# The sign bit of converted weights from a two-slope ACT function, and weight rounding at the head of a unit, in pooled attention with two MLPs

## The chip, the cores and the metric

The kernel runs on one core of one Trainium2 chip. The metric is the device time of one execution in microseconds. The core has five engines that run their own instructions in order: TensorE (PE, with the weight loads shown as PEld), VectorE (DVE), ScalarE (ACT), GpSimd (POOL) and SyncE (SP), which here only issues DMAs. They wait for each other through semaphores.

## What is computed

Attention over queries that are pooled in pairs, then an MLP with a squared ReLU, then a gated MLP without an activation:

```
q_pool = mean of two neighbouring queries            # (2, 8, 576, 64)
attn   = softmax(q_pool @ k.T / sqrt(64)) @ v        # k, v: (2, 8, 1152, 64)
x      = attn as (1152, 512)
g      = s * relu(x @ w_in)**2 + b                   # w_in: (512, 2048)
x2     = g @ w_out                                   # (2048, 512)
out    = ((x2 @ w_a) * (x2 @ w_b)) @ w_out2          # w_a, w_b: (512, 1536); w_out2: (1536, 512)
```

The weights of both MLPs arrive as float64. The result is float32.

## The kernel before

All products run on TensorE in a float32 form that rounds its operands, so each operand is split into a rounded part `h` and the rest `l`, and a product takes three matmuls: h·h, h·l, l·h (`mm3`, L542).

Attention comes first, for eight pairs of heads. Its instructions on all engines are put in order by hand: the list `SCHED` names the steps of one pair, with primes for those that run one or more pairs late, and `CV` in it is one step of weight conversion. Ten such steps lie in the last pairs and behind them.

The first MLP has 16 units of weights (columns of `w_in` or rows of `w_out`, 1024 values per partition each), the second has 12 (m = 0 to 11, a 512x128 block of `w_a` and one of `w_b`). Units are numbered through, so the second MLP begins with unit 16. A unit of the second MLP is two groups of matmuls: w = 0 makes x2·w_a, which ACT copies out as `at`; w = 1 makes x2·w_b, which VectorE multiplies by `at` into `ab`. A group is 12 blocks of three matmuls of 384 columns. The last stage multiplies `ab`, split again, by all of `w_out2`.

Each unit of weights is converted from float64 by six steps of a generator (`conv_all`, L155). The four of `conv_bits` (L136 to L146) build float32 bits in `f`: (1) ACT scales the high word, read as a float32, by 2^-112 (L139); (2) VectorE shifts it left by three (L141), which loses the sign; (3) VectorE ORs in the three top bits of the low word (L143); (4) VectorE ORs in the sign of the high word (L145). The two of `conv_split` round on GpSimd: `wh` (L150) and the rest `wl` (L152). Step five also issues the DMA of a later unit's raw weights (`unit_load`, L125), from SP's queue, into one of two `raw` buffers, which is free when the last reader of its old contents has finished.

`w_out2` is converted by a generator of its own, `w2_conv` (L711), in 12 blocks kf with 512 values per partition, through one buffer `w2raw` and one buffer `f2`. Its first load, `w2_load(0)`, is issued when the generator is first advanced.

What sets the order in the second MLP (loop at the end of the function): for each m, behind the matmuls and evacuations of w = 0, six steps of `conv` (rounding of unit m+17, then the bits of unit m+18), and behind those of w = 1 six steps of `w2_steps` (bits and rounding of block m). `unit_next` at the head of m takes the rounded weights that were made during the unit before. The rounded weights have two buffers, so `wh` of a unit can be written when TensorE has finished the unit two before. The memory of the first MLP is given back at `m1.close()` (L695), and the pool `m2`, which holds `w2raw`, `f2`, `ab` and the rounded `w_out2`, is laid over it.

Of the kernel before, what the change touches and what calls it, by code (L numbers as in the profile page):

```python
# [8 lines left out]
F32 = mybir.dt.float32  # L9
# [3 lines left out]
AF = mybir.ActivationFunctionType  # L13
ALU = mybir.AluOpType
# [27 lines left out]
def kernel(  # L42
# [14 lines left out]
    nc = tc.nc  # L57
# [52 lines left out]
    for up, c, u in order1:  # L110
        if up:
            w = w_in[:, c * 512 + u * 256:c * 512 + (u + 1) * 256]
        else:
            w = w_out[c * 512:(c + 1) * 512, u * 256:(u + 1) * 256]
# [21 lines left out]
    def conv_bits(f, raw):  # L136
        words = raw.bitcast(I32).rearrange("p (n t) -> p n t", t=2)
        lo, hi = words[:, :, 0], words[:, :, 1]
        nc.scalar.activation(out=f.bitcast(F32), in_=hi.bitcast(F32), func=AF.Copy, scale=2.0 ** -112)  # L139
        yield  # L140
        nc.vector.tensor_scalar(out=f, in0=f, scalar1=3, scalar2=None, op0=ALU.logical_shift_left)  # L141
        yield
        nc.vector.scalar_tensor_tensor(out=f, in0=lo, scalar=29, in1=f, op0=ALU.logical_shift_right, op1=ALU.bitwise_or)  # L143
        yield
        nc.vector.scalar_tensor_tensor(out=f, in0=hi, scalar=-(1 << 31), in1=f, op0=ALU.bitwise_and, op1=ALU.bitwise_or)  # L145
        yield  # L146

    def conv_split(f, h, l):
        f = f.bitcast(F32)
        nc.gpsimd.tensor_scalar(out=h, in0=f, scalar1=1.0, scalar2=0.0, op0=ALU.mult, op1=ALU.add)  # L150
        yield
        nc.gpsimd.tensor_tensor(out=l, in0=f, in1=h.bitcast(F32), op=ALU.subtract)  # L152
        yield

    def conv_all():  # L155
        for i in range(len(units)):
            f = cv_ps[i % len(cv_ps)].tile([128, 1024], I32, tag="f", name="f")
            yield from conv_bits(f, raw_t.pop(i))
            unit_load()
            p = sp_ps[i % 2]  # L160
            h, l = (p.tile([128, 1024], F32R, tag=f"w{x}", name=f"w{x}") for x in "hl")
            sp_t.append((h, l))
            yield from conv_split(f, h, l)

    conv = conv_all()

    def conv_step(n=1, steps=conv):
        for _ in range(n):
            next(steps, None)

    def unit_next():
        return sp_t.pop(0)
# [369 lines left out]
    def mm3(parts, w, x, first, last):  # L542

        (wh, wl), (xh, xl) = w, x
        for z, (a, c) in enumerate([(wh, xh), (wh, xl), (wl, xh)]):
            o = 0
            for ps in parts:
                n = ps.shape[-1]
                nc.tensor.matmul(ps, a, c[:, o:o + n], start=(first and z == 0), stop=(last and z == 2))  # L549
                o += n  # L550

    with tc.manual_schedule():
# [35 lines left out]
        def ps_tile():  # L588
            p = ps_pools[n_ps[0] % 2]
            n_ps[0] += 1  # L590
            return [p.tile([128, 512], F32, tag=f"ps{i}", name=f"ps{i}")[:, 0:NT // 3] for i in range(3)]
# [111 lines left out]
        def w2_at(x, kf):  # L703
            return w2[x][:, kf]

        def w2_load(kf):
            raw = m2_p.tile([128, DM], I64, tag="w2raw", name="w2raw")
            nc.sync.dma_start(out=raw, in_=w_out2[kf * 128:(kf + 1) * 128, :])
            return raw

        def w2_conv():  # L711
            raw = w2_load(0)
            for kf in range(KF2):
                f = m2_p.tile([128, DM], I32, tag="f2", name="f2")
                yield from conv_bits(f, raw)
                if kf + 1 < KF2:
                    raw = w2_load(kf + 1)
                yield from conv_split(f, w2_at(0, kf), w2_at(1, kf))

        w2_steps = w2_conv()  # L720
        ab = m2_p.tile([128, KF2, NT], F32, tag="ab", name="ab")
        tiles = [(b, j) for b in range(B) for j in range(4)] + [None]
        orow = [out[b * SP:b * SP + 512].rearrange("(p j) d -> p j d", j=4) for b in range(B)]
# [4 lines left out]
        def ab_split(i):  # L728
            if i >= len(chunks):
                return  # L730
            t, z = chunks[i]
            kc = slice(4 * z, 4 * z + 4)
            a = abt[i] = sp_ps[i // 2 % 2].tile([128, 2, 4, 128], F32R, tag=f"w{'hl'[i % 2]}", name="abt")
            if t is not None:
                b, j = t
                split(a[:, 0], a[:, 1], ab[:, kc, b * SP + cols(j):b * SP + cols(j) + 128], nc.scalar, nc.vector)
            else:
                for b in range(B):
                    c = slice(b * NX, (b + 1) * NX)
                    split(a[:, 0, :, c], a[:, 1, :, c], ab[:, kc, b * SP + 256:b * SP + 256 + NX], nc.scalar, nc.vector)  # L740

        for m in range(KF2):
            wh, wl = (x.rearrange("p (w k f) -> p w k f", w=2, k=4) for x in unit_next())
            if m == KF2 - 1:
                ab_split(0)
                ab_split(1)
            at = a_p.tile([128, NT], F32, tag="at", name="at")
            for w in range(2):
                ps = ps_tile()
                for kk in range(KD):  # L750
                    mm3(ps, (wh[:, w, kk], wl[:, w, kk]), (x2h[:, kk], x2l[:, kk]), kk == 0, kk == KD - 1)
                for i in range(3):
                    c = slice(i * NT // 3, (i + 1) * NT // 3)
                    if w == 0:
                        nc.scalar.copy(out=at[:, c], in_=ps[i])  # L755
                    else:
                        nc.vector.tensor_tensor(out=ab[:, m, c], in0=ps[i], in1=at[:, c], op=ALU.mult)
                conv_step(6, w2_steps if w else conv)
        conv_step(1, w2_steps)

        for i, (t, z) in enumerate(chunks):
# [49 lines left out]
```

## Time and profile before

| | |
|---|---|
| median of 3 runs | 716.09 us (715.78 to 716.54) |
| profiled execution: time / span | 716.33 us / 714.5 us |
| PE busy | 694.3 us, 97%, 4302 matmuls |
| DVE busy | 489.1 us, 68%, 911 instructions |
| ACT busy | 366.7 us, 51%, 859 |
| POOL busy | 385.8 us, 54%, 388 |
| share of the chain that ended last | PE 83%, DVE 9%, ACT 3%, POOL 2% |

Times inside the execution are counted from the start of the span. Busy time of TensorE is not its peak: matmuls are pipelined, and their durations overlap, so the distance between starts says how fast it goes. The granted clock is given as a share of full speed, 1.00 being 2.4 GHz and 0.50 1.2 GHz. Attention ends at about 271 us, the first MLP at about 475, the second MLP's units at 630 and TensorE's last matmul at 704.8 us.

### The profile page before, as it was taken

Reading aid. Unit: us, or ns where it says so; the run is one execution under the profiler, and the core shown is the slowest. Engines: PE = TensorE matmul, PEld = TensorE weight load, DVE = VectorE, ACT = ScalarE, POOL = GpSimd, SP = SyncE. Lnnn points to the kernel's source line nnn. Section 1 sums busy time; section 2 is a strip of 40 time slices with the busy share of each in tenths; the row PEclk is TensorE's granted clock in tenths of the full one; section 3 lists DMA queues with packets and bytes.
Section 4 is the critical chain, followed back from the end, with each engine's and each line's share of the span. In section 5 each row is a group of like instructions: output and inputs, shape, how many; then the busy total and the mean of one; then the engine's idle time right before and its main releaser. Section 6 shows DMA issues by size and latency. Waiting matters only on the chain.

```text
span 714.5 us, 11549 instructions
## 1 busy us (share of the span) xinstructions
PE 694.3 (97%) x4302; PEld 665.3 (93%) x4302; DVE 489.1 (68%) x911; ACT 366.7 (51%) x859; POOL 385.8 (54%) x388
## 2 busy tenths in 40 slices
PE   7999999999999989999999999999899999999994
PEld 6899999999999989999999999999899999988883
DVE  5999999999999995786386577675555546342220
ACT  5998999999999983454333224122113131222220
POOL 4879798888879764785545454231544352410000
PEclk9999999999999999999999999999999999999998
DMA  6122120312121004231313131223252430100000
GB/s 224 35 67 67 36 77 25 100 32 69 34 67 35 1 8 149 81 118 65 113 60 119 60 118 59 93 85 118 89 175 90 148 119 30 60 16 30 29 30 29
DMA packets 32443, 52.90 MB, mean 74 GB/s; under 512 B 1924, under 2 KB 15492, under 8 KB 32388
## 3 DMA queue, kind: packets, MB, share of 16 engines
q1 hardware_dynamic: 32258, 52.04, 22.2%
q8 instruction: 34, 0.56, 0.3%
q14 instruction: 21, 0.17, 0.1%
q10 hardware_dynamic: 130, 0.13, 0.1%
HBM read 49.81 MB, written 2.36 MB: 73 GB/s over the span
## 4 chain that ended last, share of the span: by engine, by line
PE 83%; DVE 9%; ACT 3%; POOL 2%; issue 2%; DMA 1%; ACTq 0%; POOLq 0%
PE ps L549 47%; PE ps L769 9%; PE pv L434 8%; PE t L400 7%; PE s L325 6%; PE s L332 3%; DVE p3l L418 2%; DVE sm L351 2%; PE t L270 1%; ACT p3h L412 1%; PE t L290 1%; DVE sm L348 1%; DVE xs L453 1%; DMA w2raw<-in_moe_w_out_dram 1%; ACT x L275 1%
## 5 line engine op out<-in xcount | busy, mean ns | idle before, releaser
L400 PE MATMUL t<-ident,e 128*128 128x128 f32 x648 | 98.5, 275 | 3.3 <-DVE p2l L418 1.5
L383 POOL TENSOR_SCALAR e<-e,sm 128x1152 f32<-128x1152 f32 x72 | 88.5, 1231 | 11.5 <-DVE sm L378 6.7
L400 PEld LDWEIGHTS t<-ident,e 128*128 128x128 f32 x648 | 75.2, 140 | 13.6 <-DVE p3l L418 2.1
L653 POOL TENSOR_SCALAR r<-r,sb_s,sb_b 128x384 f32<-128x384 f32 (+1 forms) x46 | 44.5, 979 | 54.7 <-DVE r L650 54.7
L141 DVE TENSOR_SCALAR f<-f 128x1024 int32<-128x1024 int32 (+1 forms) x40 | 30.5, 763 | 60.0 <-ACT f L139 59.9
L152 POOL TENSOR_TENSOR wl<-f,wh 128x1024 fp32r<-128x1024 f32 x28 | 69.8, 2492 | 2.2
L348 DVE TENSOR_REDUCE sm<-s 128x1 f32<-128x768 f32 x72 | 68.3, 948 | 2.0 <-PE s L325 2.0
L418 DVE TENSOR_TENSOR p3l<-t,p3h 128x512 fp32r<-128x512 f32 (+1 forms) x120 | 64.3, 554 | 7.0 <-ACT p3h L412 4.6
L549 PE MATMUL ps<-x2h,wl 128*128 128x384 f32 x288 | 66.3, 338 | 2.0 <-POOL wl L152 2.0
L769 PE MATMUL ps<-w2h,abt 128*128 128x512 f32 x216 | 67.4, 393 | 0.0
L549 PE MATMUL ps<-x2h,wh 128*128 128x384 f32 x288 | 66.2, 338 | 0.4 <-POOL wh L150 0.4
L367 ACT ACTIVATE e<-s,sm 128x768 f32<-128x768 f32 x72 | 66.5, 923 | 0.0
L549 PE MATMUL ps<-x2l,wh 128*128 128x384 f32 x288 | 66.0, 337 | 0.0
L755 ACT COPY at<-ps 128x384 f32<-128x384 f32 x36 | 14.9, 487 | 97.2 <-PE ps L549 97.2
L150 POOL TENSOR_SCALAR w2h<-f 128x512 fp32r<-128x512 f32 x12 | 8.2, 683 | 94.7 <-DVE f L145 94.7
L412 ACT CAST p3h<-t 128x512 fp32r<-128x512 f32 (+1 forms) x120 | 56.2, 485 | 6.0 <-PE t L400 3.7
L150 POOL TENSOR_SCALAR wh<-f 128x1024 fp32r<-128x1024 f32 x28 | 32.8, 1171 | 45.4 <-PE ps L549 39.8
L549 PEld LDWEIGHTS ps<-x2h,wl 128*128 128x128 f32 x288 | 51.7, 190 | 2.3 <-POOL wl L152 2.3
L549 PEld LDWEIGHTS ps<-x2h,wh 128*128 128x128 f32 x288 | 51.9, 190 | 0.7 <-POOL wh L150 0.7
L98 DVE TENSOR_TENSOR abt<-ab,abt 128x512 fp32r<-128x512 f32 (+1 forms) x30 | 19.9, 699 | 46.9 <-ACT abt L93 46.9
L549 PEld LDWEIGHTS ps<-x2l,wh 128*128 128x128 f32 x288 | 51.8, 189 | 0.0
L647 ACT ACTIVATE r<-ps 128x384 f32<-128x384 f32 (+1 forms) x46 | 20.2, 505 | 60.0 <-PE ps L549 60.0
(106 smaller groups left out, 1906.0 us busy)
## 6 DMA issues: line engine op xcount, KB each, us to landing
raw<-in_moe_w_in_dram SPq DMA_DIRECT2D x8, 1024.0 KB, 5.5
raw<-in_moe_w_out_dram SPq DMA_DIRECT2D x8, 1024.0 KB, 5.0
raw<-in_moe_w_a_dram SPq DMA_DIRECT2D x12, 512.0 KB, 3.6
raw<-in_moe_w_b_dram SPq DMA_DIRECT2D x12, 512.0 KB, 4.7
w2raw<-in_moe_w_out_dram SPq DMA_DIRECT2D x12, 512.0 KB, 3.3
vn<-in_v_dram SPq DMA_DIRECT2D x8, 576.0 KB, 3.9
kn<-in_k_dram SPq DMA_DIRECT2D x7, 576.0 KB, 3.9
qn<-in_q_dram SPq DMA_DIRECT2D x7, 512.0 KB, 3.7
```

The costliest lines, as they stand in the source:

```text
L152: nc.gpsimd.tensor_tensor(out=l, in0=f, in1=h.bitcast(F32), op=ALU.subtract)
L325: nc.tensor.matmul(ps[:, c, 0:384], w, x[:, c * 384:(c + 1) * 384], start=(z == 0), stop=(z == len(pr) - 1))
L348: nc.vector.reduce_max(small(g)[:, 0:1], SPS[g, 0][:, :, 0:384], axis=AX.XY)
L367: nc.scalar.activation(out=e_tile(g)[:, 0:768].rearrange("p (a c) -> p a c", a=2), in_=SPS.pop((g, 0))[:, :, 0:384], func=AF.Exp, bias=m[: ...
L383: nc.gpsimd.tensor_scalar(out=e, in0=e, scalar1=m[:, 6:7], scalar2=1.0, op0=ALU.mult, op1=ALU.mult)
L400: nc.tensor.transpose(ps[:, i * 128:(i + 1) * 128], E[g][:, (c0 + i) * 128:(c0 + i + 1) * 128], ident)
L412: nc.scalar.copy(out=p_dst(g)[0][:, c0:c0 + n], in_=p_src(g, z))
L418: nc.vector.tensor_tensor(out=l, in0=p_src(g, z), in1=h.bitcast(F32), op=ALU.subtract)
L434: nc.tensor.matmul(ps[:, 0:N], V[n, hd][:, c].rearrange("p a d -> p (a d)"), p, start=(t == 0), stop=(t == 2 * NC - 1))
L549: nc.tensor.matmul(ps, a, c[:, o:o + n], start=(first and z == 0), stop=(last and z == 2))
L653: nc.gpsimd.tensor_scalar(out=r2, in0=r2, scalar1=sb_s, scalar2=sb_b, op0=ALU.mult, op1=ALU.add)
L769: nc.tensor.matmul(ps, a[:, x, kk], w2_at(c, kf), start=(kf == 0 and y == 0), stop=(kf == KF2 - 1 and y == 2))
```

## The change

The first conversion step uses ACT's function Prelu, whose slope for negative inputs is alpha times that for positive ones. With alpha = 2^32 a negative value's exponent is 32 higher, which is bit 28 of the word, and the shift left by three brings this bit to the sign's place. The fourth step, the OR of the sign on VectorE, is gone; its `yield` stays, so that the count of steps is as before.

In the second MLP, two conversion steps (the rounding of the next unit's weights, with the DMA of a later unit's raw weights) stand at the head of a unit and no longer behind its first group, where four steps are left. The load of the first block of `w_out2` is issued when the generator is made, ahead of the loop and of `ab`'s allocation.

```diff
     def conv_bits(f, raw):
         words = raw.bitcast(I32).rearrange("p (n t) -> p n t", t=2)
         lo, hi = words[:, :, 0], words[:, :, 1]
-        nc.scalar.activation(out=f.bitcast(F32), in_=hi.bitcast(F32), func=AF.Copy, scale=2.0 ** -112)
+
+        nc.scalar.activation(out=f.bitcast(F32), in_=hi.bitcast(F32), func=AF.Prelu, scale=2.0 ** -112, alpha=2.0 ** 32)
         yield
         nc.vector.tensor_scalar(out=f, in0=f, scalar1=3, scalar2=None, op0=ALU.logical_shift_left)
         yield
         nc.vector.scalar_tensor_tensor(out=f, in0=lo, scalar=29, in1=f, op0=ALU.logical_shift_right, op1=ALU.bitwise_or)
         yield
-        nc.vector.scalar_tensor_tensor(out=f, in0=hi, scalar=-(1 << 31), in1=f, op0=ALU.bitwise_and, op1=ALU.bitwise_or)
         yield
...
-        def w2_conv():
-            raw = w2_load(0)
+        def w2_conv(raw):
             for kf in range(KF2):
...
-        w2_steps = w2_conv()
+        w2_steps = w2_conv(w2_load(0))
         ab = m2_p.tile([128, KF2, NT], F32, tag="ab", name="ab")
...
         for m in range(KF2):
             wh, wl = (x.rearrange("p (w k f) -> p w k f", w=2, k=4) for x in unit_next())
+            conv_step(2)
             if m == KF2 - 1:
...
-                conv_step(6, w2_steps if w else conv)
+                conv_step(*((6, w2_steps) if w else (4,)))
         conv_step(1, w2_steps)
```

## Rows read from the trace of the kernel before

**Rows 1.** Table by stretches: length, busy PE, PEld, DVE, ACT, POOL; clock; DMA, GB/s.

```profile
179.46:211.83 32.37, 32.26 (x241) 30.97 (x241) 30.76 (x74) 29.82 (x80) 27.38 (x34) 1.00 0.18 56
211.83:244.47 32.64, 32.42 (x241) 30.98 (x241) 31.55 (x75) 30.96 (x81) 27.66 (x34) 1.00 0.06 20
244.47:271.07 26.60, 24.79 (x180) 23.09 (x179) 24.95 (x56) 21.22 (x54) 19.01 (x22) 1.00 0.12 41
...
287.01:475.00 187.99, 187.93 (x1079) 186.66 (x1078) 130.76 (x179) 66.75 (x126) 97.16 (x75) 1.00 0.25 85
...
500.13:509.85 9.72, 7.34 (x32) 6.70 (x32) 5.96 (x8) 0.68 (x1) 7.64 (x6) 0.82 0.49 163
509.85:630.08 120.23, 120.23 (x695) 120.23 (x695) 56.49 (x81) 27.47 (x50) 47.18 (x35) 1.00 0.28 93
```

**Rows 2.** Chain that ended last, in order of time: start, length, what.

```profile
264.30 1.68 DVE f L145
...
280.68 1.65 DVE f L145
...
488.38 5.67 DMA w2raw<-in_moe_w_out_dram
494.13 0.67 ACT f L139
...
501.26 3.21 POOL wl L152
```

**Rows 3.** Timeline, TensorE at the stall: start, duration, idle time before it in brackets.

```profile
500.13 0.69 PE L549 MATMUL ps<-x2h,wl 128*128 128x384 f32 x3
501.23 0.80 PE L549 MATMUL ps<-x2h,wh 128*128 128x384 f32 x3 [0.41 <-POOL wh L150]
...
504.51 1.03 PE L549 MATMUL ps<-x2h,wl 128*128 128x384 f32 x3 [1.96 <-POOL wl L152]
...
509.85 0.68 PE L549 MATMUL ps<-x2h,wh 128*128 128x384 f32 x3
```

**Rows 4.** Table by stretches, two microseconds behind the gap.

```profile
506.00:508.00 2.00, 2.00 (x8) 2.00 (x7) 0.19 (x1) 0.00 (x0) 1.64 (x2) 0.50 0.68 202
```

**Rows 5.** Timeline, SP's queue of DMA issues.

```profile
487.36 0.37 SPq L132 DMA_DIRECT2D raw<-in_moe_w_a_dram  x1
...
488.38 8.73 SPq L708 DMA_DIRECT2D w2raw<-in_moe_w_out_dram  x2
```

**Rows 6.** Timeline, VectorE from the first MLP's end through unit 16.

```profile
476.92 3.38 DVE L98 TENSOR_TENSOR x2l<-xacc,x2h 128x384 fp32r<-128x384 f32 x3
...
486.06 1.23 DVE L145 SCALAR_TENSOR_TENSOR f<-raw,f 128x1024 int32<-128x1024 int32 x1
488.02 1.49 DVE L757 TENSOR_TENSOR ab<-ps,at 128x384 f32<-128x384 f32 x3 [0.73 <-PE ps L549]
```

**Rows 7.** Timeline, GpSimd in an undisturbed unit of the second MLP.

```profile
520.86 0.62 POOL L150 TENSOR_SCALAR w2h<-f 128x512 fp32r<-128x512 f32 x1 [9.11 <-DVE f L145]
...
523.97 2.42 POOL L152 TENSOR_TENSOR wl<-f,wh 128x1024 fp32r<-128x1024 f32 x1
```

**Rows 8.** Timeline, TensorE beside the two L145 of the chain.

```profile
266.19 0.31 PE L434 MATMUL pv<-p3l,v 128*128 128x320 f32 x1
266.73 0.63 PE L400 MATMUL t<-ident,e 128*128 128x128 f32 x4 [0.23 <-DVE p2l L418]
...
283.10 0.42 PE L549 MATMUL ps<-xa_h,wl 128*128 128x288 f32 x2
283.73 0.53 PE L549 MATMUL ps<-xa_h,wh 128*128 128x288 f32 x2 [0.20 <-DVE r L650]
```

**Rows 9.** Groups by line: busy time, mean ns of one, idle time before and its releaser.

```profile
L145 DVE SCALAR_TENSOR_TENSOR f<-raw,f 128x1024 int32<-128x1024 int32 x28 | 36.7, 1310 | 0.9
...
L139 ACT ACTIVATE f<-raw 128x1024 f32<-128x1024 f32 x28 | 32.3, 1154 | 2.4 <-POOL wl L152 2.4
...
L93 ACT ACT_TABLE_LOAD x1 | 1.3, 1283 | 0.7 <-PEq L795 0.7
```

## The prediction

> **What bounds the kernel now.** I read the table by stretches first, because the mean busy share says nothing about which stage a change touches. From the first MLP on TensorE is the bound: in 287 to 475 us it is busy for 187.93 of 187.99 us at a granted clock of 1.00, and in 510 to 630 us for all 120.23 us [rows 1]. In there a cheaper VectorE step is worth nothing by itself: VectorE is idle for half of the later stretch. One stretch stands out, 500.13 to 509.85 us: TensorE 7.34 of 9.72 us, clock 0.82 [rows 1].
>
> Second, the chain of waits, to see what holds TensorE there. It runs from the first DMA of `w2raw` (issued 488.38, landed 494.05) over the ACT conversion at 494.13 and VectorE and GpSimd to `wl` at 501.26, ready at about 504.5 [rows 2]. Third, TensorE's own order of time. A block of three matmuls, one 128x384 tile by three parts, comes every 0.52 us; from the block at 500.13 to the one at 509.85 there are ten steps, which should take 5.20 us and take 9.72 [rows 3]. So 4.52 us are lost at this one place. Of that, 9.72 - 7.34 = 2.38 us is idle time, and the other 2.14 us is the clock: after the gap ahead of 504.51 it is granted at 0.50, the 1.2 GHz level, in 506 to 508 us [rows 3, 4].
>
> Earlier the chain also runs over the operation that is removed, L145: at 264.30 for 1.68 us, at the end of the attention, and at 280.68 for 1.65 us, in the first unit of the first MLP [rows 2]. These two places and the stall at 500 us are where the change can act. What TensorE does elsewhere is its own work.
>
> **The stall at 500 us, part by part.** The change moves `w2_load(0)` to ahead of all steps of the second MLP. Before, SP's queue holds the raw load of a later unit first. That load waits for its buffer, whose last reader is L145 of unit 18 (486.06 + 1.23 = 487.29), goes at 487.36, and `w2_load(0)` follows at 488.38 [rows 5, 6]. After, nothing of this loop is ahead of it in SP's queue. It must still wait for memory of the first MLP that `w2raw` is laid over; the last user of that memory which I see is `x2l<-xacc` on VectorE, ending at 476.92 + 3.38 = 480.30 [rows 6]. So the issue moves from 488.38 to 480.30 at the latest, and with the slowest landing seen, 494.05 - 488.38 = 5.67 us, the data are there by 485.97. The raw load queued behind it on SP loses nothing: its buffer comes free at 486.03 at the earliest, when L143 ends.
>
> What is late next? The ACT conversion of `f2` (0.67 us) can then run at 486.0. VectorE's two steps on it stand behind the three products `ab` of unit 16, 488.02 to 489.51 [rows 6], so the bits of `f2` are done at about 490.7. In an undisturbed unit `w2h` starts at 520.86 and the `wl` behind it ends at 523.97 + 2.42 = 526.39, 5.53 us later [rows 7]. So `wl` of unit 18 is ready at 490.7 + 5.5 = 496.2. TensorE's third block of unit 18 wants it at 500.13 + 3 x 0.52 = 501.69. The slack is 5.5 us, the stall goes whole, and with it the clock's fall, as nothing later in the loop waits at all [rows 1]. Gain 4.52 us.
>
> The removal helps at the same place, so the gain does not hang on the load alone. It frees the raw buffer 1.23 us earlier and takes 0.69 us out of the `f2` chain; 504.5 would become about 502.5 even with the old order of loads. Also, GpSimd's `wl` takes 3.21 us in the stall against 2.42 us undisturbed [rows 2, 7], while VectorE runs L143 and L145 beside it. The Trainium skill's SBUF — State Buffer (Who interferes with whom) says that GpSimd and a VectorE operation with two SBUF inputs take one shared port pair by an exclusive lock, and that the loser blocks. By that rule the removal alone would give back most of the excess, and the stall would be short even where the load did not move; the rows show a slowdown but not who held what.
>
> The rest of the second edit I cost at nothing: `conv_step(2)` at a unit's head emits the raw DMA and the two GpSimd roundings that stood behind the first half's evacuation. GpSimd's order stays wh, wl, w2h, w2l; SP's order stays raw, raw, w2raw; ACT and VectorE get nothing from these two steps. The cover is that each queue meets the same neighbours as before.
>
> **The removal elsewhere.** 28 L145 of about 1.31 us and 12 shorter ones leave VectorE [rows 9], some 45 us of busy time, but only two of them stand on the path. At 264.30, taking 1.68 us off the chain does not give 1.68 us: TensorE is at work until 266.19 plus one step of 0.15, and its next transposes start at 266.73 [rows 8]. So 0.39 us come free, and then TensorE is what is late. Bounds: 0, if the next GpSimd normalisation is late instead, to 1.81 us, all idle time of TensorE in 244.47 to 271.07 [rows 1]. I take 0.39, the row nearest to the removed step. At 280.68, the block at 283.73 would have come at 283.10 + 0.27 = 283.37 [rows 8]; 0.36 us is lost there. GpSimd's 576-column step on `r` and the ACT rounding behind it end shortly before L145 does, and become late next; I take 0.3, between 0 and 0.5.
>
> The Prelu replaces a Copy of equal shape: 1.15 us for 1024 columns [rows 9]. No row shows a Prelu, so I bound it by neighbours. One such ACT step, with its first VectorE step, was added to the period 211.83 to 244.47, which takes 32.64 us against 32.37 for the one before: 0.27 us for 1.15 us of ACT [rows 1]. If Prelu took twice as long, it would cost 0.3 to 1.15 us there, and nothing later, where ACT is idle for most of each unit; a faster one would give back 0.27 at most. I take 0, because Relu, Copy and Exp of this kernel follow their sizes and not their function.
>
> Sum: 4.52 + 0.39 + 0.3 = 5.2 us. The profiled run took 716.33 us with a span of 714.5; it becomes 711.1, its span 709.3. The median of the runs, 716.09, lies 0.24 lower, so the forecast is 710.9 us.
>
> **Rivals.** (1) The stall is cured only in part. The `f2` chain starts earlier but something else on GpSimd or ACT keeps `wl` late, say 1 us of idle time (1.81 us in 244.47 to 271.07 left the clock at 1.00 [rows 1]), and the attention's end gives nothing: 716.09 - 3.5 = 712.6. For it: the chain has seven links on four engines. Against it: 5.5 us of slack.
>
> (2) Prelu needs another table on ACT than Exp. The profile has one table load, 1283 ns, at the start, with Exp, Copy and Relu all run under it [rows 9]. A Prelu outside that set would put a load before the conversion at 215 us and one after it, where ACT is busy for 30.96 of 32.64 us [rows 1], 2 x 1.28 = 2.57 us at most, and a third at 272 us, in ACT's idle time: 710.9 + 2.6 = 713.5. What speaks against it is that a two-slope function is as cheap as Relu, which is in the set. The Trainium skill's ScalarE: Activation LUTs (What ACT_TABLE_LOAD costs) gives 2.66 us for a switch, load and drain; by that figure two switches are 5.3 us and the result an estimated 716.2, no change. Its load alone agrees with the row's 1283 ns; the drain no row here shows. The same page (Table sets) has cheap functions in every set, without naming this one.
>
> (3) Slower: SP's in-order queue. `w2_load(0)` now stands ahead of the raw loads, and its memory might come free later than I read. The chain from landing to `wl` is 504.47 - 494.05 = 10.4 us, less the removed 0.69, so 9.7. If the data land at L, TensorE loses L + 9.7 - 501.69 + 2.14 us; against the 4.52 + 0.69 us gained otherwise, it turns slower from L = 495 on, an issue at about 489.4. Held until unit 17 ends at 500.65, it lands at 506.32 and TensorE loses 16.5 us: 710.9 + 16.5 = 727.4. For it: the tile is allocated earlier than before, so it lies elsewhere. Against it: no user of the first MLP's memory is seen after 480.30, 9 us before the deciding point.
>
> (4) The change does not do what it says: the load stays as late as it was, and the contention keeps `wl` late. Only the two small places remain: 716.09 - 0.7 = 715.4.
>
> **How the numbers follow.** Forecast 710.9, chance 0.78, with its own range from 709.5 (0.39 replaced by 1.81 us) to 711.6 (both small places give nothing). Rival 1 has 0.12, rival 2 0.05, rival 4 0.03 and rival 3 0.02. The range runs from 709.5 to rival 1's 712.6; what lies above it, 713.5 and more, has 0.10. A measurement of this kernel can tell about 0.2%, 1.4 us, from no change; the bound is 714.7. Forecast and rivals 1 and 2 are faster, 0.95; rival 4 is the same, 0.03; rival 3 slower, 0.02.
>
> **What would show it.** In the changed profile the first `w2raw` DMA should be issued by 480.3 us on the old scale, `wl` of unit 18 should end some 5 us before TensorE wants it, and every unit of the second MLP should take 12.48 us at clock 1.00 with no wait of TensorE on GpSimd. The attention's end should be about 0.4 us earlier, not 1.7. Only one table load should stand on ACT, and the Prelu should take about 1.15 us. The forecast is wrong if the load goes out at 488 or later and the stall stays, or if a second table load appears before 220 us.

## The result, and the profile after

The changed kernel takes 709.64 us (median, 709.48 to 710.83) against 716.25 us: a ratio of 0.9915, 95% interval 0.9901 to 0.993. It is 6.6 us faster. The forecast was 710.9 us with a range from 709.5 to 712.6; the gain was forecast as 5.2 us. The profiled run took 709.62 us, its span is 707.8 us.

The two traces start differently by chance: the first conversion on ACT begins at 215.41 us before and at 214.91 after, although nothing is changed ahead of it. In the twelve profiled runs told of here it lies between 213.64 and 216.24, and a second run of the changed kernel (g4 below) has 215.59. So stages are compared by their own lengths, between marks that all kernels have: A the first conversion on ACT, B the nine transposes that begin at 263.85 before, C the first block of the first MLP, D its first block of 384 columns, E the rounding `wh` of unit 17 on GpSimd (it starts when TensorE ends the first MLP), F the first and G the last matmul of the last stage. Each length is a difference of two starts in a timeline.

| us | A to B | B to C | C to D | D to E | E to F | F to G | A to G |
|---|---|---|---|---|---|---|---|
| before | 48.44 | 7.22 | 15.94 | 188.38 | 154.69 | 74.32 | 488.99 |
| after | 48.53 | 6.76 | 15.83 | 187.13 | 150.19 | 74.33 | 482.77 |
| gain | -0.09 | 0.46 | 0.11 | 1.25 | 4.50 | -0.01 | 6.22 |

The other 0.5 us of the profiled runs' difference is the chance start. The stall in the second MLP was forecast at 4.52 us and gave 4.50; the attention's end was forecast at 0.39 and gave 0.46; the first unit 0.3 and gave 0.11. The 1.25 us in the first MLP (D to E) were not forecast. The forecast is right in the main, but one term is missing from its sum.

The table by stretches of the kernel after; its columns are those of [rows 1]. The first stretch answers to that from 287.01 there, the second to those from 500.13 and 509.85 together, though it ends 0.15 us ahead of mark F:

```profile
286.00:472.80 186.80, 186.80 (x1079) 186.80 (x1078) 109.12 (x163) 66.12 (x125) 93.38 (x74) 1.00 0.27 87
...
497.90:623.20 125.30, 125.30 (x724) 125.30 (x724) 42.12 (x68) 27.39 (x50) 50.54 (x38) 1.00 0.31 101
```

The second line holds what was the stall and the units behind it: TensorE is busy for all of it, at clock 1.00, where [rows 1] and [rows 4] had 0.82 and 0.50. The chain that produced the stall, in the kernel after, from the timelines of VectorE, SP, GpSimd and TensorE (start, duration; idle time before in brackets):

```profile
474.68 3.38 DVE L98 TENSOR_TENSOR x2l<-xacc,x2h 128x384 fp32r<-128x384 f32 x3
...
478.15 0.34 SPq L708 DMA_DIRECT2D w2raw<-in_moe_w_out_dram  x1
...
488.49 0.62 POOL L150 TENSOR_SCALAR w2h<-f 128x512 fp32r<-128x512 f32 x1 [11.79 <-DVE f L144]
...
491.59 2.41 POOL L152 TENSOR_TENSOR wl<-f,wh 128x1024 fp32r<-128x1024 f32 x1
...
497.89 0.69 PE L549 MATMUL ps<-x2h,wl 128*128 128x384 f32 x3
498.42 0.70 PE L549 MATMUL ps<-x2h,wh 128*128 128x384 f32 x3
498.96 0.68 PE L549 MATMUL ps<-x2l,wh 128*128 128x384 f32 x3
499.48 0.68 PE L549 MATMUL ps<-x2h,wl 128*128 128x384 f32 x3
```

The load of `w2raw` goes out at 478.15, when the last `x2l<-xacc` has ended (474.68 + 3.38 = 478.06), and not behind another raw load as in [rows 5]. `wl` of unit 18 ends at 494.00. TensorE wants it at 499.48: the slack is 5.5 us, as forecast, and the four blocks follow each other in 0.52 to 0.54 us, where [rows 3] has 1.10 us for the first step and 3.28 us for the next two together.

Groups of the kernel after, which answer to [rows 9]:

```profile
L140 ACT ACTIVATE f<-raw 128x1024 f32<-128x1024 f32 x28 | 32.4, 1156 | 2.4 <-POOL wl L152 2.4
...
L93 ACT ACT_TABLE_LOAD x1 | 1.3, 1283 | 0.7 <-PEq L795 0.7
```

The Prelu takes 1156 ns where the Copy took 1154, and there is still one table load.

### The profile page after: what moved, and what is told of

It is laid out like the page before. It is cut to its first block, busy times and chain, and to the rows that moved or that the text cites. A ratio compares the mean times of both kernels' runs of the same rounds, so it can differ in the third digit from the quotient of the medians.

```text
span 707.8 us, 11508 instructions
## 1 busy us (share of the span) xinstructions
PE 690.8 (98%) x4302; PEld 663.9 (94%) x4302; DVE 440.4 (62%) x871; ACT 366.3 (52%) x859; POOL 380.0 (54%) x388
## 4 chain that ended last, share of the span: by engine, by line
PE 86%; DVE 7%; ACT 3%; issue 2%; POOL 1%; DMA 0%; ACTq 0%
PE ps L549 49%; PE ps L769 10%; PE pv L434 9%; PE t L400 7%; PE s L325 6%; PE s L332 3%; DVE p3l L418 2%; DVE sm L351 1%; PE t L270 1%; PE t L290 1%; ACT p3h L412 1%; DVE xs L453 1%; DVE sm L348 1%; ACT x L275 1%; ACT e L367 1%
## 5 line engine op out<-in xcount | busy, mean ns | idle before, releaser
L653 POOL TENSOR_SCALAR r<-r,sb_s,sb_b 128x384 f32<-128x384 f32 (+1 forms) x46 | 40.9, 901 | 55.4 <-DVE r L650 55.4
L142 DVE TENSOR_SCALAR f<-f 128x1024 int32<-128x1024 int32 (+1 forms) x40 | 26.4, 660 | 65.9 <-ACT f L140 65.8
L418 DVE TENSOR_TENSOR p2l<-t,p2h 128x512 fp32r<-128x512 f32 x96 | 50.6, 548 | 1.2 <-ACT p2h L412 1.1
```

The costliest lines, as they stand in the source:

```text
L418: nc.vector.tensor_tensor(out=l, in0=p_src(g, z), in1=h.bitcast(F32), op=ALU.subtract)
L653: nc.gpsimd.tensor_scalar(out=r2, in0=r2, scalar1=sb_s, scalar2=sb_b, op0=ALU.mult, op1=ALU.add)
```

## The experiments

All lengths below are between the marks of the table above; times are medians of several rounds beside the kernel before on the same chip.

**e1, the removal alone.** The edit to the kernel before:

```diff
-        nc.scalar.activation(out=f.bitcast(F32), in_=hi.bitcast(F32), func=AF.Copy, scale=2.0 ** -112)
+        nc.scalar.activation(out=f.bitcast(F32), in_=hi.bitcast(F32), func=AF.Prelu, scale=2.0 ** -112, alpha=2.0 ** 32)
...
-        nc.vector.scalar_tensor_tensor(out=f, in0=hi, scalar=-(1 << 31), in1=f, op0=ALU.bitwise_and, op1=ALU.bitwise_or)
```

> Only the first edit: Prelu in place of Copy, and the sign's OR on VectorE taken out. The second MLP's loop and the first load of w_out2 stand as before. Theory A (the removal is worth 0.46 us at the attention's end, 0.12 at the first unit, 1.24 in units 1 to 3 of the first MLP, and the stall at 500 us needs the load's move): about 1.8 us are gained outside the stall, and of the stall's 4.50 us some 0 to 1 us stay, because the chain from w2raw to wl becomes 1.26 + 0.69 us shorter than the 2.8 us by which it was late: 710.0 to 711.5 us. Rival B (the removal alone cures the stall whole, by taking VectorE off GpSimd's back): 709.6 us, as the changed kernel. Rival C (the load's place is all that matters for the stall): 716.25 - 1.8 = 714.4 us.

**e2, the early load alone.**

```diff
-        def w2_conv():
-            raw = w2_load(0)
+        def w2_conv(raw):
...
-        w2_steps = w2_conv()
+        w2_steps = w2_conv(w2_load(0))
```

> Only the first load of w_out2 is moved ahead of the second MLP's loop; Copy, the sign's OR and the loop are as before. Theory A: the stall goes whole, 4.5 us, and nothing else moves: 716.25 - 4.5 = 711.75 us, and in the first MLP the three late block starts near 294, 306 and 320 us stay. Rival C' (the early load alone does not do it, since GpSimd's wl stays slow beside VectorE): 713 to 716 us.

**e3, the loop's edit alone.**

```diff
+            conv_step(2)
             if m == KF2 - 1:
...
-                conv_step(6, w2_steps if w else conv)
+                conv_step(*((6, w2_steps) if w else (4,)))
```

> Only the loop's edit: two conversion steps at the head of a unit, four behind its first group; Copy, the sign's OR and the place of the first load of w_out2 in the generator are as before. Theory A: each engine's queue keeps its order, so nothing changes: 716.25 us within 0.5, with the stall at 500 us as before. Rival D (GpSimd's rounding starts earlier when it stands ahead of the unit's matmuls): 711.7 us, the stall gone.

**e4, the changed kernel with the sign's OR put back.**

```diff
+        nc.vector.scalar_tensor_tensor(out=f, in0=hi, scalar=-(1 << 31), in1=f, op0=ALU.bitwise_and, op1=ALU.bitwise_or)
         yield
```

> The changed kernel with the sign's OR put back on VectorE behind the Prelu (it ORs a sign that is already there). Theory A: the OR's 28 + 12 instructions cost 1.8 us at the attention's end and in the first MLP, and nothing in the second MLP: 709.64 + 1.8 = 711.5 us, equal to the load's move alone within 0.3, because a Prelu costs what a Copy costs. Rival E (a Prelu is slower than a Copy and the removal's worth is larger than it looks): 712.3 us or more. Rival F (the 1.24 us in the first MLP come from an earlier start of the kernel and not from the OR): 710.2 us.

These four ran on one chip, where the kernel before took 715.69 us:

| | time | B to C | C to D | D to E | E to F | A to G |
|---|---|---|---|---|---|---|
| e1, removal alone | 709.98 | 6.75 | 15.82 | 187.13 | 150.33 | 482.81 |
| e2, load alone | 710.96 | 7.23 | 15.95 | 188.38 | 150.19 | 484.58 |
| e3, loop alone | 715.06 | 7.22 | 15.95 | 188.41 | 154.69 | 489.05 |
| e4, changed, with the OR | 711.72 | 7.21 | 15.96 | 188.39 | 150.19 | 484.56 |

The ratios to the kernel before are 0.9913 (0.9899 to 0.9926), 0.9926 (0.9914 to 0.9939), 0.9992 (0.9983 to 1.0001) and 0.9938 (0.9926 to 0.9951).

The loop's edit is worth nothing: e3 has the lengths of the kernel before, the stall included. e4 equals e2 to 0.02 us from A to G, so a Prelu costs what a Copy costs (the medians of the whole time differ by 0.76 us, but the two ratios' intervals overlap, and A lies 1.81 us later in e4's profiled run). The gains outside the second MLP come with the removal (e1) and go with it (e4). The stall, though, is cured twice: by the load alone (150.19) and by the removal alone but for 0.14 us (150.33). My theory A, that the stall needs the load's move, was wrong there, though the 0 to 1 us that it left over hold the 0.14; rival B is nearly right in time. `wh` on the chain of the kernel before, and then two timelines of e1, GpSimd and TensorE, show how narrowly:

```profile
499.17 2.01 POOL wh L150
```

```profile
494.91 1.50 POOL L149 TENSOR_SCALAR wh<-f 128x1024 fp32r<-128x1024 f32 x1
496.49 3.25 POOL L151 TENSOR_TENSOR wl<-f,wh 128x1024 fp32r<-128x1024 f32 x1
...
499.25 0.69 PE L548 MATMUL ps<-x2l,wh 128*128 128x384 f32 x3
499.80 0.80 PE L548 MATMUL ps<-x2h,wl 128*128 128x384 f32 x3
500.44 0.68 PE L548 MATMUL ps<-x2h,wh 128*128 128x384 f32 x3
```

`wl` ends at 499.74 and TensorE's block that wants it starts at 499.80; the next comes 0.64 us later and not 0.52. Before, `wl` was 2.78 us late (504.47 against 501.69). Counted from mark E it ends 29.08 us later before and 26.29 in e1, that is 2.79 us earlier, and so the lateness is made up to the last tenth. Of the 2.79 us, 1.25 come from the raw buffer that is free earlier: ACT's conversion of `w2raw` starts 18.74 us behind E before, and 17.49 in e1 (at 490.94). From there to the start of `w2h` 0.73 us are gone with the removed step. The other 0.8 us are GpSimd's: `w2l` gives 0.31 us and `wh`, which takes 1.50 us where it took 2.01, gives 0.54, and `wl` takes some hundredths back. So VectorE was taken off GpSimd's back, as rival B has it, but that is less than a third of the cure.

The prediction drew from the shared port pair (Trainium skill, SBUF — State Buffer, Who interferes with whom) that the removal alone would give back most of the excess of `wl`. The conclusion, a short stall, came true, but not by `wl`: it takes 3.25 us in e1, where it took 3.21. The timelines show a likely reason. Before, the sign's OR still runs beside the first 1.0 us of `wl` (to 502.24); in e1 the OR of the low word (495.54, 1.94 us) does so for the same 1.0 us.

So the 4.5 us belong to neither edit: either earns them, the load with 5.5 us of slack, the removal with none.

**f1, another operation in the OR's place.** Where did the first MLP's 1.25 us come from: VectorE's time, or what its operation does to GpSimd? To the changed kernel, with `mx` a new tile of one column:

```diff
         nc.vector.scalar_tensor_tensor(out=f, in0=lo, scalar=29, in1=f, op0=ALU.logical_shift_right, op1=ALU.bitwise_or)
         yield
+        nc.vector.reduce_max(mx[:, 0:1], f.bitcast(F32), axis=AX.X)
         yield
```

> The changed kernel with another VectorE instruction where the sign's OR stood: a maximum over f (128x1024 to 128x1) into a tile that nobody reads. It keeps VectorE for about as long (128x768 takes 0.95 us in attention, so some 1.2 us) but reads one operand and writes one column. Theory P (the 1.24 us of late block starts in the first MLP come from GpSimd being slowed beside VectorE's operation with two SBUF operands: its step on r takes 5.09 us for three against 3.74 in the changed kernel): the late starts near 294, 306 and 319 us do not come back, GpSimd's three steps on r stay near 3.7 us; only the 0.46 us at the attention's end come back, where VectorE's own queue is late: first conversion to last matmul 483.2 us against 482.8 changed and 484.6 with the OR. Rival O (VectorE's occupancy is what counts): the late starts come back, 484.6 us.

It took 708.53 us. D to E is 186.96: the late blocks don't come back, though the 28 maxima keep VectorE for 34.1 us, nearly as long as the 28 ORs with 36.7 [rows 9]. The timelines of GpSimd (three steps on `r`) and VectorE near 299 us, first in the kernel before, with the sign's OR, then in f1, with the maximum:

```profile
298.93 5.09 POOL L653 TENSOR_SCALAR r<-r,sb_s,sb_b 128x384 f32<-128x384 f32 x3
...
301.13 1.57 DVE L145 SCALAR_TENSOR_TENSOR f<-raw,f 128x1024 int32<-128x1024 int32 x1
```

```profile
296.56 3.36 POOL L655 TENSOR_SCALAR r<-r,sb_s,sb_b 128x384 f32<-128x384 f32 x3
...
298.76 1.22 DVE L147 TENSOR_REDUCE mx<-f 128x1 f32<-128x1024 f32 x1
```

With the OR beside them the three steps take 5.09 us and end 1.3 us after it; with the maximum there they take 3.36 us, and in the kernel after, with neither, 3.74. The maximum is 0.35 us shorter than the OR here, which is little beside the 1.73 us that GpSimd's steps are shorter. The one reads two operands from SBUF and writes 1024 columns, the other reads one and writes one column. This is theory P: the OR's price in the first MLP is what it takes from GpSimd, whose `r` ACT's `gh` and VectorE's `gl` wait for, and behind them the reading of the accumulators that TensorE's next matmuls need. The Trainium skill's SBUF — State Buffer (Who interferes with whom) has GpSimd blocked by a VectorE operation with two SBUF inputs; that the maximum with one input leaves GpSimd alone agrees with it. Which of operands and output counts, this run does not separate.

At the attention's end I expected the 0.46 us to come back, and they did not (B to C 6.77). There the two operations differ more in length: the maximum took 1.21 us at 264.44, the OR 1.68 on the chain at 264.30 [rows 2]. Behind either of them VectorE makes `p2l`, which TensorE's next transposes wait for [rows 8]. VectorE's timeline before, and then those of VectorE and TensorE in f1:

```profile
265.90 1.47 DVE L418 TENSOR_TENSOR p2l<-t,p2h 128x512 fp32r<-128x512 f32 x3
```

```profile
265.57 1.48 DVE L420 TENSOR_TENSOR p2l<-t,p2h 128x512 fp32r<-128x512 f32 x3
...
266.56 0.60 PE L402 MATMUL t<-ident,e 128*128 128x128 f32 x4
```

Counted from mark B, `p2l` starts after 2.05 us before and after 1.50 in f1; the transposes come after 2.88 and 2.49, and in the kernel after, with nothing in the OR's place, after 2.47. In f1 they stand 0.15 us behind TensorE's last product, without a wait: `p2l` is just early enough. So the price at this place is VectorE's time after all, and 0.41 of the 0.46 us are these transposes: the OR is too long for the gap, and the maximum is not. Why the OR takes 1.68 us here and 1.23 at 486.06 [rows 6] was not tested.

**f3, the empty step moved.** The kernel after has one long wait of TensorE left in this part, 1.27 us, and one of 0.2. To the changed kernel:

```diff
         nc.vector.tensor_scalar(out=f, in0=f, scalar1=3, scalar2=None, op0=ALU.logical_shift_left)
         yield
+        yield
         nc.vector.scalar_tensor_tensor(out=f, in0=lo, scalar=29, in1=f, op0=ALU.logical_shift_right, op1=ALU.bitwise_or)
         yield
-        yield
```

> The changed kernel with the empty step ahead of the OR of the low word and not behind it, so that in the attention's end this OR (L144) stands where the sign's OR stood, some 2 us later, and in both MLPs nothing moves but within a group of four steps. Theory Q (TensorE's one remaining wait there, 1.27 us at 263.44, is caused by the OR, beside which GpSimd's small sum takes 1.31 us and not 0.29): the wait falls to about 0.3 us, and the OR delays the p2l casts by some 0.4 us as the sign's did: 0.4 to 0.8 us faster than the changed kernel, 482.0 to 482.4 us from the first conversion to the last matmul. Rival R (the wait belongs to the chain of softmax itself): no gain, 482.8 to 483.3 us.

It took 708.25 us; A to B is 47.44 and B to C 7.22, A to G 482.14: 0.6 us less than the kernel after, theory Q. The timelines of GpSimd's small sum and TensorE's transposes in the kernel after; then the sum in f3's timeline, and the list of f3's waits on TensorE from 240 to 640 us (in total, times, longest):

```profile
261.59 1.31 POOL L374 TENSOR_SCALAR sm<-sm 128x1 f32<-128x1 f32 x1 [1.27 <-ACT e L367]
...
263.44 1.18 PE L400 MATMUL t<-ident,e 128*128 128x128 f32 x9 [1.27 <-DVE p2l L418]
```

```profile
262.86 0.29 POOL L374 TENSOR_SCALAR sm<-sm 128x1 f32<-128x1 f32 x1 [1.28 <-ACT e L367]
```

```profile
PE t L400 <- DVE p2l L418: 0.3, 1, 0.3
PE t L400 <- POOL e L383: 0.2, 1, 0.2
```

A sum of one column takes 1.31 us because VectorE's OR of the low word, 1.22 us from 261.54, runs beside it, and 0.29 us without. Moved to where the sign's OR had been, the same OR costs what that one did, 0.46 us, so 0.6 us are left of 1.09.

**g, a column of constants.** In f1 the last stage, which has no conversion in it, took 73.25 us and not 74.33. f1 has one more tile, of one column, made as the last of the constants and ahead of all the larger tiles that follow. Three kernels with an idle tile (`pad`, n columns, set to zero once), and the changed kernel again, on one chip, where the kernel before took 714.88 us:

```diff
     sb_b = const.tile([128, 1], F32, name="sb_b")
+    pad = const.tile([128, n], F32, name="pad")
...
         make_identity(nc, ident)
+        nc.vector.memset(pad, 0.0)
```

> The changed kernel once more, so that it stands on one chip beside the two kernels below. All theories: 709.6 us within 0.7; first conversion to last matmul 482.8 us, of which the last stage (630.08 to 704.40 us before) takes 74.3 us.

> The changed kernel with one more column of constants in SBUF (128x1, set to zero once at the start, read by nobody), as the run with the maximum had for its result. In that run the last stage took 73.25 us and not 74.3, with no waits in either. Theory S (where the tiles behind it lie in SBUF sets how fast TensorE's 512-column matmuls follow each other): the last stage takes 73.25 us again, and the time from the first conversion to the last matmul is 481.3 us. Rival T (it came from the forty extra instructions on VectorE, or from chance): 74.3 us and 482.8 us.

> As the run with one more column, with 16 columns (64 bytes per partition). Theory S with any shift doing it: last stage 73.25 us. Theory S with the address counting in a coarse step: 74.3 us, as without it, or a third value between. Rival T: 74.3 us.

> Both together: the empty step ahead of the low word's OR, and the one column of constants. If the two gains are independent, the wait of 1.27 us stays at 0.3 us and the last stage at 73.25 us: 0.6 + 1.4 us below the changed kernel on the same chip, about 707.6 us. Rival: the padding's gain is chance, 709.0 us.

| | time | D to E | E to F | F to G | A to G |
|---|---|---|---|---|---|
| g4, changed kernel | 709.70 | 187.13 | 150.19 | 74.32 | 482.66 |
| g1, one column | 708.46 | 186.93 | 150.03 | 73.25 | 481.33 |
| g3, 16 columns | 711.59 | 188.85 | 151.47 | 74.30 | 485.65 |
| g2, one column, and f3's edit | 707.56 | 186.94 | 150.03 | 73.25 | 480.72 |

Theory S holds so far: an idle tile changes how fast matmuls follow each other, and its size decides, since g1 and g3 have the same instructions but for the width of one memset. That it acts through the places of the tiles behind it is the obvious reading; the places themselves no run shows. It goes both ways, which I had not expected: 16 columns cost 3.0 us. The last stage in g4 and g1, by the table by stretches:

```profile
623.93:698.25 74.32, 74.32 (x324) 60.65 (x324) 20.55 (x33) 18.88 (x36) 2.60 (x2) 1.00 0.08 29
```

```profile
623.53:696.78 73.25, 73.25 (x324) 60.62 (x324) 20.57 (x33) 18.89 (x36) 2.60 (x2) 1.00 0.08 29
```

The same 324 matmuls at the same clock, with TensorE busy throughout, follow each other in 230 or 227 ns. Which tile's place it is, and why, stays open. g1 is also f1 without its maximum: with 186.93 us from D to E, against 186.96, it shows that the maximum itself costs nothing there, and that f1's 0.17 us below the kernel after belong to the column. g2 beats both kernels: 707.56 us, a ratio of 0.9895 (0.9882 to 0.9909) to the kernel before.

## Why the prediction was right, and where it was not

**The stall: right in place, size and mechanism.** 4.50 us for 4.52. The release of memory at the end of `x2l<-xacc`, the slack of 5.5 us and the return of the clock came as worked out. The sentence on the removal alone (504.5 becomes 502.5, so 0.8 us late) was 0.9 us off: the chain's own steps were shortened rightly, by 1.92 us, but GpSimd's gain was not put into the number, and it was named at `wl`, where it did not come. There a row was misread too: L143 does not run beside `wl` in the stall, it ends at 500.25, a microsecond before `wl` starts.

**The attention's end: right. The first unit: right in sign, too large.** At the attention's end 0.46 for 0.39, and not the 1.68 us of the chain's piece. In the first unit 0.11 for 0.3. The chain of the kernel after has there what the prediction named as late next, GpSimd's `r` and ACT's rounding:

```profile
278.36 2.05 POOL r L653
280.43 0.68 ACT gh L93
281.14 0.88 DVE gl L98
282.02 0.68 DVE r L650
```

The chain of the kernel before has the same `gl` behind the sign's OR:

```profile
282.33 0.67 DVE gl L98
```

Counted from VectorE's `r` before them (278.36 before, 277.49 after), `gl` starts after 3.97 and 3.65 us: these 0.32 us are the forecast 0.3. But `gl` itself takes 0.88 us and not 0.67, and so 0.21 us go back. The prediction has no term for that. GpSimd's `wl`, which now begins beside `gl`, is longer too, 2.76 us and not 2.40; no experiment tests what the two do to each other.

**The first MLP: the step that failed.** From 187.93 of 187.99 us busy [rows 1] I concluded that a cheaper VectorE step "is worth nothing by itself" in this stretch and that "What TensorE does elsewhere is its own work", and set the removal at nothing there. It was worth 1.25 us. The busy time is modelled from matmuls that overlap, and small waits of the weight loads vanish in it. The next column of the same row has them: the weight loads are busy for 186.66 of 187.99 us before, and in the kernel after for all of 186.80. Two views of the kernel before that the prediction did not use for this stretch show where: the waits of the weight loads from 284 to 325 us, and the timelines of the weight loads and of TensorE at 306 us.

```profile
PEld ps L549 <- DVE r L650: 1.2, 5, 0.3
```

```profile
306.15 0.19 PEld L549 LDWEIGHTS ps<-xa_h,wh 128*128 128x128 f32 x1 [0.23 <-DVE r L650]
306.61 0.19 PEld L549 LDWEIGHTS ps<-xa_h,wh 128*128 128x128 f32 x1 [0.28 <-DVE r L650]
```

```profile
305.89 1.16 PE L549 MATMUL ps<-xa_h,wh 128*128 128x384 f32 x3
306.89 0.68 PE L549 MATMUL ps<-xa_l,wh 128*128 128x384 f32 x3
```

The block at 305.89 has 1.16 us of busy time where its neighbour has 0.68: the wait counts as busy. The list of waits of the kernel after has none in this stretch, e1 has the same 187.13 us from D to E, and e2 and e4, which keep the OR, have the waits of the kernel before. Between starts of blocks the loss is 0.11 us after 293.27, 0.48 after 305.89 and 0.64 after 318.86, together 1.23 of the 1.25 us. This is a term that was missing, not one that was mis-sized, and it is why the time lies near the range's lower end: 5.2 + 1.25 = 6.45 us. That end had been worked out from another place, all 1.81 us of idle time at the attention's end, so it is partly luck that the time lies inside the range.

**The Prelu and the rest of the loop's edit: right, at nothing** (e4 against e2, and e3). A to B is 0.09 us longer after than before, but 48.45 us in e1, which has the Prelu too.

**The rivals.** Rival 2 did not happen: one table load. What the Trainium skill's ScalarE: Activation LUTs (What ACT_TABLE_LOAD costs) gives for a switch no run here shows. That cheap functions lie in every set (Table sets there, which does not name this one) fits Prelu beside Exp under one load, but these runs show it for one set only. Rival 3 did not: SP held the load no longer than the last reader of the old memory. Rivals 1 and 4 would have needed the load or GpSimd to stay late. Neither did; e1, where the load kept its old place in the queue, still has 0.14 us of the stall.

## What to carry to other kernels

Before an edit is set at nothing because TensorE is "busy throughout", look at the busy time and the waits of its weight loads and at the distance between starts of its blocks: 0.1 to 0.6 us per place hid in a stretch with 0.06 us of idle time. An operation's price may be on another engine: taking one away from VectorE paid in the first MLP through GpSimd. A stand-in of another length does not tell what an operation costs in a gap that only one of them fits. Where a stall has two causes in series, price each cure alone; here either of them earned nearly all 4.5 us, and together no more.

## What was not expected of the hardware

An idle tile of one column, made ahead of the large tiles, made the last stage's matmuls follow each other in 227 and not 230 ns (73.25 against 74.32 us for 324), and one of 16 columns lengthened the first MLP from 187.13 to 188.85 us; so two kernels that differ by a fraction of a per cent may differ by nothing but the size of a tile that nobody reads. And a one-column sum on GpSimd takes 1.31 us with VectorE's OR of two operands beside it, and 0.29 us without (f3).
